# A cross network on one core: first rows in three loads, the tail's inputs moved up, padded bias sums, and the tail corner as 32x32 tiles

## The chip, the core and the metric

The kernel runs on one core of a Trainium2 chip. The metric is the device time of one execution in microseconds (us), the median of several runs. One further execution was recorded by the hardware profiler; all durations of single instructions below come from it. The core's engines are TensorE (PE in the profile, and PEld for its weight loads), VectorE (DVE), ScalarE (ACT), GpSimd (POOL) and SyncE (SP, which here only issues transfers).

## What is computed

Six layers of a cross network over 4096 rows of 416 features, all in bf16:

```python
B, F, D, L = 4096, 26, 16, 6
Din = min(F * D, 1024)          # 416
# x0: [4096, 416]   ws: [6, 416, 416]   bs: [6, 416]
def reference(x0, ws, bs):
    x = x0
    for l in range(ws.shape[0]):
        x = x0 * (x @ ws[l] + bs[l]) + x
    return x
```

The kernel uses that x is x0 times a running sum S: it keeps S in PSUM, adds each layer's product to it, and gets the next x as x0 * (S + sum of the biases).

## The kernel before

**Layout.** Features lie on partitions, rows on the free axis. The 416 features are three chunks of 128 (the "main" part, `CH`) and a tail of 32. The 4096 rows are four blocks of 1024 (`s`), and each block has two halves of 512. The sum S of a block stands in PSUM banks 0 to 5 (three chunks, two halves) and, for the tail, in banks 6 and 7 (`T_BANK`), where four quarters of 256 rows lie on the four groups of 32 partitions.

**One layer of one block** is a fixed piece of TensorE work, and there are 24 of them (six layers, four blocks; the last one is done in another form). In order:

- `main` for the first half: nine calls, each four matmuls of 128 rows of the array by 32 columns, which run side by side and stream 512 columns each;
- `tail_rows`, the 32 tail inputs: here the array is used as four groups of 32 rows, with 128 columns each. The part `first` does two chunks of 128 outputs. The part `second` does the third chunk (groups 0 and 2, 512 streamed columns each) and the *corner*, tail inputs to tail outputs, 32 by 32 (groups 1 and 3);
- `tail_outs`, main inputs to tail outputs, again 128 by 32;
- `main` for the second half.

VectorE takes every finished bank out of PSUM (`leave`, L417), ScalarE and GpSimd do the same for the tail (`leave_tail`, L427 and L440) and copy it into a second, swapped order (`swap`), because groups 1 and 3 of the array hold the other quarters' tail inputs as well.

**The corner.** `wc_sb` holds, for each layer, the 32x32 corner of the weights placed in a 128-column block that is zero elsewhere. GpSimd makes it: one memset of the whole tile (L249) and four copies for each group of layers (`corner`, L255): layer 0 early, layer 1 after layer 0 of the first block, layers 2 to 5 after layer 1. Each use is two matmuls of 256 columns in row group 1 and two in row group 3, with the zeros adding nothing to the other quarters.

**The head.** TensorE first runs 14 matmuls on constants (`fill`). The first 512 rows come by two plain loads of 256 rows (`load_rows`: rows 0 to 255 on SP's queue, 256 to 511 on ACT's) and are transposed on TensorE (L488), with six copies out of PSUM into `x0T_sb` (DVE L503, four; ACT L498, two). All later rows come by transposing loads on SP's queue (L204). In layer 0 of the first block the weights come in three pieces, and the nine `main` calls go chunk by chunk (`k`): after the first, `bias_sums` (16 small matmuls, weights `bsa_sb` of 7 partitions, against `u_sb`; ACT copies the result to `cb_sb`, L522); after the second, `tail_in(0)` (16 matmuls that transpose the tail inputs; ACT copies them to `x0t_sb`, L388).

**Order.** A small planner (`Plan`) keeps each engine's instructions in program order and puts in the semaphore waits; TensorE never passes a waiting instruction. SP issues, in order: rows 0 to 255, the three pieces of layer 0's weights, the tail inputs `xtl0` of rows 512 to 1023, the transposing load of rows 512 to 1023, and then the weights of layer 1 and on. ACT issues rows 256 to 511, the biases `bs`, and layer 0's tail weights `wt0`, and only then loads its function table.

Of the kernel before, what the change touches and what calls it, by code (L numbers as in the profile page):

```python
# [118 lines left out]
def bass_standalone__dcn_v2_cross__recsys_kernel(  # L119
# [6 lines left out]
    B, D = x0.shape  # L126
# [8 lines left out]
    G = SB // 4  # L135
# [6 lines left out]
    with ExitStack() as es:  # L142
# [5 lines left out]
        wt_sb = sb("wt_sb", [128, L, D])  # L148
        wc_sb = sb("wc_sb", [128, L, 2, 128])
        xin_sb = sb("xin_sb", [128, 4, D])  # L150
# [16 lines left out]
        dummy_sb = sb("dummy_sb", [128, 8])  # L167
        bsa_sb = sb("bsa_sb", [L + 1, D])
        u_sb = sb("u_sb", [L + 1, L])
        cb_sb = sb("cb_sb", [128, NC + 1, L], FP32)  # L170
# [23 lines left out]

        def load_rows(queue, i):
            load(queue, xin_sb[:, 2 * i:2 * i + 2, :], x0_v[:, 2 * i:2 * i + 2, :], "xin%d" % i, [("xin", i)])

# [9 lines left out]

        load_rows("sync", 0)
        load_rows("scalar", 1)
        for k in CH:  # L210
            load("sync", w_sb[:, 0, k, :], ws[0, 128 * k:128 * k + 128, :], "w0_%d" % k, [("w", 0, k)])
        load("scalar", bsa_sb[1:L + 1, :], bs[:, :], "bs", [("bs",)])
        load(
            "scalar", wt_sb[:, 0, :], ws[0, DF:D, :].unsqueeze(0).to_broadcast([4, DR, D]), "wt0", [("wt", "wt0")]
        )
        load("sync", xtl_sb[:, 4:JS, :], x0_v[:, 4:JS, DF:D], "xtl0", [("xtl", 0)])
        load_transposed(0, H, SB)
# [8 lines left out]
        for s in range(1, NS):  # L226
# [14 lines left out]
        )  # L241
        P.add("gpsimd", lambda e: e.memset(bsa_sb[0:1, :], 1.0), writes=[("bs1",)])
        P.add(
            "gpsimd", lambda e: e.affine_select(
                out=u_sb[:, :], in_=ones_sb[0:L + 1, 0:L], pattern=[[1, L]],
                compare_op=ALU.is_ge, fill=0.0, base=1, channel_multiplier=-1,
            ), reads=[("ones",)], writes=[("u",)],
        )
        P.add("gpsimd", lambda e: e.memset(wc_sb[:, :, :, :], 0.0), writes=[("wc", "wt%d" % i) for i in range(3)])  # L249

        def corner(a, b, name):
            for g in range(4):
                p = quad(g | 1)
                P.add(
                    "gpsimd", lambda e, p=p, g=g: e.tensor_copy(  # L255
                        out=wc_sb[p, a:b, g % 2, quad(g)], in_=wt_sb[p, a:b, DF:D]
                    ), reads=[("wt", name), ("wc", name)], writes=[("wc", name, g)], shifts=True,
                )


# [47 lines left out]
        def tail_rows(s, l, start):  # L308
            src, key = src_tail(s, l)
            keys = [("wt", wkey(l)), key, key + ("swapped",)]  # L310

            def rows(pe, q, h, m, begin):
                for part in range(2):
                    if q % 2 == 0:
                        if part:
                            break
                        dst, rhs = ps[:, bank(h, m), :], src[quad(q), :, :]
                    else:
                        dst, rhs = ps[:, bank(h, m), part * G:(part + 1) * G], src[quad(q), 1 - part, :]
                    ins = mm(  # L320
                        pe, dst, wt_sb[quad(q), l, m * 128:(m + 1) * 128], rhs, begin and part == 0, (32 * q, 0)
                    )
                return ins

            def first(pe):
                for q in range(4):
                    h, m = divmod(q, 2)
                    ins = rows(pe, q, h, m, l == 0 and h == 1)
                return ins

            def second(pe):
                for q in range(4):
                    h = q // 2
                    if q % 2 == 0:
                        ins = rows(pe, q, h, 2, l == 0 and h == 1)
                    else:
                        for part in range(2):
                            ins = mm(
                                pe, ps[:, T_BANK[h], 0:G], wc_sb[quad(q), l, part, :], src[quad(q), 1 - part, :],
                                start and part == 0, (32 * q, 0),  # L340
                            )
                return ins

            P.add("tensor", first, reads=keys, adds=[("ps", bank(h, m)) for h in HALVES for m in range(2)])
            P.add(
                "tensor", second, reads=keys + [("wc", wkey(l), g) for g in range(4)],
                adds=[("ps", bank(h, 2)) for h in HALVES] + [("ps", T_BANK[h]) for h in HALVES],
            )
# [18 lines left out]
        def tail_in(s):  # L367
            def fn(pe):
                for o in range(2 if s == 0 else 1):
                    for r in range(2):  # L370
                        for g in range(4):
                            j = 2 * (g ^ o) + r
                            src = xin_sb[:, j, DF:D] if s == 0 and j < 4 else xtl_sb[:, s * JS + j, :]
                            b, c = (7, o * G) if s == 0 else (T_BANK[0], G)
                            ins = mm(
                                pe, ps[quad(g), b, c + r * 128:c + (r + 1) * 128], src, ident[:, :],
                                s == 0 and o == 0 and r == 0, (0, 32 * g),
                            )
# [3 lines left out]
            P.add(  # L382
                "tensor", fn, reads=[("ident",), ("xtl", 0 if s == 0 else 1)] + ([("xin", 0), ("xin", 1)] if s == 0 else []),
                adds=[("ps", b)],
# [95 lines left out]
        B_BANK = 6  # L480
        fill(14)
        for i in range(2):
            for c in CH:
                b = HEAD_BANKS[i][c]

                def fn(pe, i=i, c=c, b=b):
                    for j in range(2):
                        ins = pe.transpose(  # L488
                            out=psT[:, b, j * 128:(j + 1) * 128],
                            in_=xin_sb[:, 2 * i + j, c * 128:(c + 1) * 128], identity=ident[:, :],  # L490
                        )
                    return ins

                P.add("tensor", fn, reads=[("xin", i), ("ident",)], adds=[("ps", b)])
                dst, src = x0T_sb[:, c, i * 256:(i + 1) * 256], psT[:, b, 0:256]
                if c == 1:
                    P.add(
# [30 lines left out]

        corner(0, 1, "wt0")
        for s in range(NS):  # L530
            for l in range(L):
# [3 lines left out]
                if s == 0 and l == 0:  # L535
                    for k in CH:
                        for m in CH:
                            main(s, l, 0, m, k)
                        if k == 0:
                            bias_sums()  # L540
                        if k == 1:
                            tail_in(0)
                    tail_rows(s, l, True)
# [14 lines left out]
                if l == 2 and s < NS - 1:  # L558
                    keep_tail_in(s + 1)
                if s == 0 and l == 0:  # L560
                    corner(1, 2, "wt1")
                if s == 0 and l == 1:
                    corner(2, L, "wt2")
                if l == 1 and s > 0:
# [156 lines left out]
```

## Time and profile before

| | |
|---|---|
| median of 3 runs | 129.16 us (128.88 to 129.17) |
| profiled execution, its own time | 129.15 us |
| its span, first to last instruction | 127.9 us |
| DVE busy | 98.2 us (77% of the span) |
| POOL busy | 39.6 us (31%) |
| DMA reads and writes | 4.07 MB and 3.41 MB of HBM |

The span is what the profiler saw between the program's first and last instruction; the remaining 1.25 us of the profiled time lie around it. A row of the timeline gives the start in us, the length in us, the engine, the line of the code, the operation, output and inputs, the shape, and how many instructions the row takes together; in square brackets stands how long the engine had been idle and what ended that. Matmuls overlap one another, so the length of a matmul row is longer than the time between the starts of two of them; what sets the pace is the distance of the starts.

The first matmuls of the program are slower than the later ones, which the timeline shows in their starts: the 14 matmuls of `fill` stream 256 columns each and begin at 0.83 us, one about every 0.21 us.

```profile
0.83 3.15 PE L270 MATMUL ps<-const-bfloat16-1.0 128*128 128x256 bf16 x14 [0.83 <-PEq L706]
```

### The profile page before, as it was taken

The numbers are of one execution on the slowest core, as the hardware profiler recorded it, in microseconds if no ns is written. First come the engines' busy times: TensorE is split into PE (matmuls) and PEld (weight loads), VectorE is DVE, ScalarE is ACT, GpSimd is POOL, SyncE is SP. The second block draws the span as 40 slices with busy tenths as digits, with TensorE's granted clock in tenths as the row PEclk, the third lists the DMA queues.
The fourth block names the chain that finished last, engine by engine and source line by source line (L and its number), as shares of the span: only waits on it lengthen the run. The fifth ranks groups of instructions, "written<-read, shape, count | busy, mean of one in ns | idle before, by whom it ended". The sixth has DMA issues, their size and how long they took to land.

```text
span 127.9 us, 5334 instructions
## 1 busy us (share of the span) xinstructions
PE 124.4 (97%) x2426; PEld 64.7 (51%) x2426; DVE 98.2 (77%) x150; ACT 50.1 (39%) x112; POOL 39.6 (31%) x88
## 2 busy tenths in 40 slices
PE   7999999999999999999999999999999999999991
PEld 5545445545545545545545545545555555455660
DVE  0329779679779779788788797797797797797973
ACT  1534226356405224354513243373422252253820
POOL 7025364034014053043122152241221351340550
PEclk9999999999999999999999999999999999999999
DMA  3987999997739307000019208000009606100016
GB/s 106 205 201 175 161 262 273 172 204 149 253 67 143 65 19 258 5 0 5 0 33 192 52 0 265 7 5 0 5 0 129 142 5 233 38 0 5 0 38 233
DMA packets 34054, 13.12 MB, mean 103 GB/s; under 512 B 25322, under 2 KB 34032, under 8 KB 34032
## 3 DMA queue, kind: packets, MB, share of 16 engines
q1 hardware_dynamic: 33328, 12.25, 45.8%
q10 hardware_dynamic: 704, 0.54, 1.3%
q8 instruction: 19, 0.31, 1.0%
q14 instruction: 3, 0.02, 0.0%
HBM read 4.07 MB, written 3.41 MB: 58 GB/s over the span
## 4 chain that ended last, share of the span: by engine, by line
PE 97%; ACT 0%; DVE 0%; issue 0%
PE ps L262 93%; PE ps L270 2%; PE ps L488 1%; ACT x0t_sb L388 0%; DVE o_sb L652 0%
## 5 line engine op out<-in xcount | busy, mean ns | idle before, releaser
L417 DVE SCALAR_TENSOR_TENSOR xT_sb<-ps,cb_sb,x0T_sb 128x512 bf16<-128x512 f32 x120 | 80.8, 743 | 19.5 <-PE ps L262 19.5
L262 PE MATMUL ps<-xT_sb,w_sb 128*32 128x512 bf16 (+1 forms) x1596 | 84.6, 364 | 0.0
L262 PEld LDWEIGHTS ps<-xT_sb,w_sb 128*32 128x32 bf16 x1596 | 40.8, 97 | 37.2 <-issue 4.0
L427 ACT ACTIVATE t_sb<-ps,cb_sb 64x256 f32<-64x256 f32 x46 | 21.6, 470 | 51.3 <-PE ps L262 51.0
L440 POOL TENSOR_TENSOR xt_sb<-t_sb,x0t_sb 128x256 bf16<-128x256 f32 x20 | 13.4, 672 | 64.1 <-ACT t_sb L427 64.1
L404 ACT ACTIVATE xt_sb<-xt_sb 32x256 bf16<-32x256 bf16 x38 | 15.7, 414 | 15.3 <-POOL xt_sb L440 15.1
L262 PE MATMUL ps<-x0T_sb,w_sb 128*32 128x512 bf16 (+1 forms) x336 | 18.9, 368 | 0.0
L406 POOL COPY xt_sb<-xt_sb 32x256 bf16<-32x256 bf16 x38 | 14.9, 392 | 2.4
L417 DVE SCALAR_TENSOR_TENSOR xo_sb<-ps,cb_sb,x0T_sb 128x512 bf16<-128x512 f32 x18 | 12.1, 743 | 2.5 <-PE ps L262 2.5
L262 PEld LDWEIGHTS ps<-x0T_sb,w_sb 128*32 128x32 bf16 x336 | 8.4, 97 | 7.6 <-issue 0.6
L262 PE MATMUL ps<-xt_sb,wt_sb 32*128 32x512 bf16 (+1 forms) x152 | 11.8, 326 | 0.0
L262 PE MATMUL ps<-xt_sb,wc_sb 32*128 32x256 bf16 x76 | 7.4, 268 | 0.0
L262 PEld LDWEIGHTS ps<-xt_sb,wt_sb 32*128 32x128 bf16 x152 | 2.5, 91 | 8.4 <-DVE xT_sb L417 6.4
L440 POOL TENSOR_TENSOR xot_sb<-t_sb,x0t_sb 128x256 bf16<-128x256 f32 x3 | 2.0, 672 | 9.9 <-ACT t_sb L427 9.9
L262 PE MATMUL ps<-w_sb,xT_sb 128*32 128x416 bf16 (+1 forms) x60 | 5.1, 339 | 0.0
L404 ACT ACTIVATE x0t_sb<-x0t_sb 32x256 bf16<-32x256 bf16 x12 | 4.9, 410 | 0.1
L652 DVE TENSOR_TENSOR o_sb<-ps,xr_sb 128x416 bf16<-128x416 f32 x6 | 3.4, 588 | 1.3 <-PE ps L262 1.0
L255 POOL COPY wc_sb<-wt_sb 32x32 bf16<-32x32 bf16 (+1 forms) x12 | 2.8, 233 | 4.7 <-DMA wt_sb<-in_ws_dram 4.1
L270 PE MATMUL ps<-const-bfloat16-1.0 128*128 128x256 bf16 x14 | 3.1, 418 | 0.8 <-PEq L706 0.8
L262 PEld LDWEIGHTS ps<-xt_sb,wc_sb 32*128 32x128 bf16 x76 | 3.7, 93 | 0.2
L503 DVE COPY x0T_sb<-ps 128x256 bf16<-128x256 bf16 x4 | 1.1, 292 | 3.4 <-PE ps L488 3.2
L449 ACT ACTIVATE sS_sb<-ps,cb_sb 128x512 bf16<-128x512 f32 x5 | 3.0, 692 | 0.0
(41 smaller groups left out, 33.6 us busy)
## 6 DMA issues: line engine op xcount, KB each, us to landing
out_dram<-o_sb SPq DMA_DIRECT2D x3, 832.0 KB, 4.4
w_sb<-in_ws_dram SPq DMA_DIRECT2D x5, 312.0 KB, 4.3
xr_sb<-in_x_dram SPq DMA_DIRECT2D x1, 832.0 KB, 5.3
wt_sb<-in_ws_dram SPq DMA_DIRECT2D x4, 104.0 KB, 2.9
out_dram<-o_sb SPq DMA_DIRECT2D x2, 208.0 KB, 2.2
w_sb<-in_ws_dram SPq DMA_DIRECT2D x3, 104.0 KB, 3.4
xin_sb<-in_x_dram ACTq DMA_DIRECT2D x1, 208.0 KB, 3.2
xin_sb<-in_x_dram SPq DMA_DIRECT2D x1, 208.0 KB, 2.9
```

The lines of the kernel that those rows point to most:

```text
L255: "gpsimd", lambda e, p=p, g=g: e.tensor_copy(out=wc_sb[p, a:b, g % 2, quad(g)], in_=wt_sb[p, a:b, DF:D]), reads=[("wt", name), ("wc", nam ...
L262: return pe.matmul(dst, lhsT=lhsT, rhs=rhs, start=start, stop=True, skip_group_check=True, tile_position=pos,)
L270: ins = pe.matmul(ps[:, 7, 0:256], lhsT=const[:, 0:128], rhs=const, start=True, stop=True)
L404: fn = lambda e, d=dst, s=src: e.activation(out=d, in_=s, func=ACTF.Copy)
L406: fn = lambda e, d=dst, s=src: e.tensor_copy(out=d, in_=s)
L417: "vector", lambda e: e.scalar_tensor_tensor(out=dst, in0=ps[:, bank(h, c), :], scalar=cb_sb[:, c, l:l + 1], in1=x0T_sb[:, c, o:o + H], op ...
L427: "scalar", lambda e, p=p, h=h: e.activation(out=dst[p, :], in_=ps[p, T_BANK[h], 0:G], func=ACTF.Identity, bias=cb_sb[p, NC, l:l + 1]), re ...
L440: "gpsimd", lambda e: e.tensor_tensor(out=dst, in0=t, in1=x0t_sb[:, s, 0, :], op=ALU.mult),
L449: fn = lambda e: e.activation(out=o, in_=i, func=ACTF.Identity, bias=b)
L488: ins = pe.transpose(out=psT[:, b, j * 128:(j + 1) * 128], in_=xin_sb[:, 2 * i + j, c * 128:(c + 1) * 128], identity=ident[:, :],)
L503: "vector", lambda e, d=dst, s=src: e.tensor_copy(out=d, in_=s),
L652: "vector", lambda e: e.tensor_tensor(out=o_sb[:, jj, :], in0=ps[:, b, 0:D], in1=xr_sb[:, j, :], op=ALU.mult), reads=[("ps", b), ("xr",)], ...
```

## The change

Four things are changed together.

- The first 512 rows come in three loads: rows 0 to 127 on SP's queue, 128 to 255 and 256 to 511 on ACT's. The transposes run row block by row block; of the six copies out of PSUM, five are now DVE's and one ACT's. `fill` has 12 matmuls.
- The tail inputs `xtl0` are loaded on ACT's queue (third, ahead of `wt0`) and no longer on SP's. In layer 0 of the first block `tail_in(0)` stands after the first chunk, and `bias_sums` after the second.
- `bsa_sb` and `u_sb` have 128 partitions. DVE clears `bsa_sb` and sets its first row to one; the biases are loaded on GpSimd's queue, after the clearing.
- The corner uses the tail weights where they lie, as tiles of 32 by 32 of the array: two matmuls of 256 columns in row group 1, into two column groups, and two in row group 3. They stand behind both 512-column matmuls of `second`. `wc_sb`, its memset and its copies are gone.

```diff
-        load_rows("sync", 0)
-        load_rows("scalar", 1)
+        load_rows("sync", 0, 1)
+        load_rows("scalar", 1, 2)
+        load_rows("scalar", 2, 4)
         for k in CH:
             load("sync", w_sb[:, 0, k, :], ws[0, 128 * k:128 * k + 128, :], "w0_%d" % k, [("w", 0, k)])
-        load("scalar", bsa_sb[1:L + 1, :], bs[:, :], "bs", [("bs",)])
+        load("scalar", xtl_sb[:, 4:JS, :], x0_v[:, 4:JS, DF:D], "xtl0", [("xtl", 0)])
         load(
             "scalar", wt_sb[:, 0, :], ws[0, DF:D, :].unsqueeze(0).to_broadcast([4, DR, D]), "wt0", [("wt", "wt0")]
         )
-        load("sync", xtl_sb[:, 4:JS, :], x0_v[:, 4:JS, DF:D], "xtl0", [("xtl", 0)])
         load_transposed(0, H, SB)
...
-        P.add("gpsimd", lambda e: e.memset(bsa_sb[0:1, :], 1.0), writes=[("bs1",)])
+        P.add("vector", lambda e: e.memset(bsa_sb[:, :], 0.0), writes=[("bs0",)])
+        P.add("vector", lambda e: e.memset(bsa_sb[0:1, :], 1.0), reads=[("bs0",)], writes=[("bs1",)])
+        P.add("gpsimd", lambda e: e.dma_start(bsa_sb[1:L + 1, :], bs[:, :]), reads=[("bs0",)], writes=[("bs",)], dma="bs")
...
-        P.add("gpsimd", lambda e: e.memset(wc_sb[:, :, :, :], 0.0), writes=[("wc", "wt%d" % i) for i in range(3)])
...
             def second(pe):
-                for q in range(4):
+                for q in (0, 2, 1, 3):
                     h = q // 2
                     if q % 2 == 0:
                         ins = rows(pe, q, h, 2, l == 0 and h == 1)
                     else:
-                        for part in range(2):
+                        for o in range(2):
+                            g = q ^ o
                             ins = mm(
-                                pe, ps[:, T_BANK[h], 0:G], wc_sb[quad(q), l, part, :], src[quad(q), 1 - part, :],
-                                start and part == 0, (32 * q, 0),
+                                pe, ps[quad(g), T_BANK[h], 0:G], wt_sb[quad(q), l, DF:D], src[quad(q), o, :],
+                                start, (32 * q, 32 * g),
                             )
...
-        fill(14)
-        for i in range(2):
+        fill(12)
+        for j in range(4):
+            i, r = divmod(j, 2)
             for c in CH:
                 b = HEAD_BANKS[i][c]
...
-                if c == 1:
+                if i and c == 2:
                     P.add(
                         "scalar", lambda e, d=dst, s=src: e.activation(out=d, in_=s, func=ACTF.Copy),
...
-        corner(0, 1, "wt0")
...
                         if k == 0:
-                            bias_sums()
-                        if k == 1:
                             tail_in(0)
+                        if k == 1:
+                            bias_sums()
...
-                if s == 0 and l == 0:
-                    corner(1, 2, "wt1")
-                if s == 0 and l == 1:
-                    corner(2, L, "wt2")
```

`tail_in` also sets the start flag on two more groups of the PSUM bank for later blocks, because the corner no longer writes them; it adds no instruction.

More of the change, by code (lines that the diff above doesn't have):

```diff
@@ L148, in bass_standalone__dcn_v2_cross__recsys_kernel @@
         wt_sb = sb("wt_sb", [128, L, D])
-        wc_sb = sb("wc_sb", [128, L, 2, 128])
         xin_sb = sb("xin_sb", [128, 4, D])
@@ L167, in bass_standalone__dcn_v2_cross__recsys_kernel @@
         dummy_sb = sb("dummy_sb", [128, 8])
-        bsa_sb = sb("bsa_sb", [L + 1, D])
-        u_sb = sb("u_sb", [L + 1, L])
+        bsa_sb = sb("bsa_sb", [128, D])
+        u_sb = sb("u_sb", [128, L])
         cb_sb = sb("cb_sb", [128, NC + 1, L], FP32)
@@ L193, in load_main, with load_rows @@
             )
-        def load_rows(queue, i):
-            load(queue, xin_sb[:, 2 * i:2 * i + 2, :], x0_v[:, 2 * i:2 * i + 2, :], "xin%d" % i, [("xin", i)])
+        def load_rows(queue, a, b):
+            load(queue, xin_sb[:, a:b, :], x0_v[:, a:b, :], "xin%d" % a, [("xin", j) for j in range(a, b)])
         def load_tail_weights(a, b, name):
@@ L241, in bass_standalone__dcn_v2_cross__recsys_kernel @@
         )
-        P.add("gpsimd", lambda e: e.memset(bsa_sb[0:1, :], 1.0), writes=[("bs1",)])
+        P.add("vector", lambda e: e.memset(bsa_sb[:, :], 0.0), writes=[("bs0",)])
+        P.add("vector", lambda e: e.memset(bsa_sb[0:1, :], 1.0), reads=[("bs0",)], writes=[("bs1",)])
+        P.add("gpsimd", lambda e: e.dma_start(bsa_sb[1:L + 1, :], bs[:, :]), reads=[("bs0",)], writes=[("bs",)], dma="bs")
         P.add(
             "gpsimd", lambda e: e.affine_select(
-                out=u_sb[:, :], in_=ones_sb[0:L + 1, 0:L], pattern=[[1, L]],
+                out=u_sb[:, :], in_=ones_sb[:, 0:L], pattern=[[1, L]],
                 compare_op=ALU.is_ge, fill=0.0, base=1, channel_multiplier=-1,
@@ L248, in bass_standalone__dcn_v2_cross__recsys_kernel @@
         )
-        P.add("gpsimd", lambda e: e.memset(wc_sb[:, :, :, :], 0.0), writes=[("wc", "wt%d" % i) for i in range(3)])
[L251 to L258, printed above, removed]
         def mm(pe, dst, lhsT, rhs, start, pos=None):
@@ L345, in tail_rows @@
             P.add(
-                "tensor", second, reads=keys + [("wc", wkey(l), g) for g in range(4)],
+                "tensor", second, reads=keys,
                 adds=[("ps", bank(h, 2)) for h in HALVES] + [("ps", T_BANK[h]) for h in HALVES],
@@ L376, in fn @@
                                 pe, ps[quad(g), b, c + r * 128:c + (r + 1) * 128], src, ident[:, :],
-                                s == 0 and o == 0 and r == 0, (0, 32 * g),
+                                o == 0 and r == 0 and (s == 0 or g >= 2), (0, 32 * g),
                             )
@@ L382, in tail_in @@
             P.add(
-                "tensor", fn, reads=[("ident",), ("xtl", 0 if s == 0 else 1)] + ([("xin", 0), ("xin", 1)] if s == 0 else []),
+                "tensor", fn, reads=[("ident",), ("xtl", 0 if s == 0 else 1)] + ([("xin", j) for j in range(4)] if s == 0 else []),
                 adds=[("ps", b)],
@@ L480, in bass_standalone__dcn_v2_cross__recsys_kernel @@
         B_BANK = 6
-        fill(14)
-        for i in range(2):
+        fill(12)
+        for j in range(4):
+            i, r = divmod(j, 2)
             for c in CH:
                 b = HEAD_BANKS[i][c]
[L486 to L494, printed above, removed]
+                P.add(
+                    "tensor", lambda pe, j=j, r=r, c=c, b=b: pe.transpose(
+                        out=psT[:, b, r * 128:(r + 1) * 128], in_=xin_sb[:, j, c * 128:(c + 1) * 128], identity=ident[:, :]
+                    ), reads=[("xin", j), ("ident",)], adds=[("ps", b)],
+                )
+                if r == 0:
+                    continue
                 dst, src = x0T_sb[:, c, i * 256:(i + 1) * 256], psT[:, b, 0:256]
-                if c == 1:
+                if i and c == 2:
                     P.add(
@@ L539, in bass_standalone__dcn_v2_cross__recsys_kernel @@
                         if k == 0:
+                            tail_in(0)
+                        if k == 1:
                             bias_sums()
-                        if k == 1:
-                            tail_in(0)
                     tail_rows(s, l, True)
```

## The prediction

> **What bounds it now.** I read the page first (who is busy), then the chain of waits (what set the end), then the timeline around one tail stage, and the head.
>
> ```profile
> PE 124.4 (97%) x2426; PEld 64.7 (51%) x2426; DVE 98.2 (77%) x150; ACT 50.1 (39%) x112; POOL 39.6 (31%) x88
> ...
> PE 97%; ACT 0%; DVE 0%; issue 0%
> PE ps L262 93%; PE ps L270 2%; PE ps L488 1%; ACT x0t_sb L388 0%; DVE o_sb L652 0%
> ```
>
> TensorE sets the end; nothing else has a percent of the chain. Told in order of time, the chain leaves TensorE just once between the first transposes and the end:
>
> ```profile
> 5.25 2.34 PE ps L262 x56
> 7.59 0.02 issue
> 7.61 0.61 ACT x0t_sb L388
> 8.22 0.05 issue
> 8.27 117.00 PE ps L262 x2240
> ```
>
> From 8.27 on, one unbroken run of 117 us. So only two things can move the time: when that run begins, and how long TensorE needs for the repeated work in it. Work taken from GpSimd is worth nothing unless TensorE waited for it.
>
> The repeated work that changes is the tail stage. One of its 23 instances (the corner rows count 76+16 = 92 matmuls, four a stage), on PE, from two windows:
>
> ```profile
> 42.36 0.39 PE L262 MATMUL ps<-xT_sb,w_sb 128*32 128x512 bf16 x4
> ...
> 42.68 0.60 PE L262 MATMUL ps<-xt_sb,wt_sb 32*128 32x512 bf16 x7
> 42.92 0.27 PE L262 MATMUL ps<-xt_sb,wc_sb 32*128 32x256 bf16 x1
> 42.92 0.37 PE L262 MATMUL ps<-xt_sb,wt_sb 32*128 32x512 bf16 x1
> 42.93 0.38 PE L262 MATMUL ps<-xt_sb,wc_sb 32*128 32x256 bf16 x3
> 43.23 0.29 PE L262 MATMUL ps<-xT_sb,w_sb 128*32 128x256 bf16 x4
> ```
>
> How long 512 columns stream: 36 of the main matmuls, nine rounds of four, fill 2.12 us with a length of 0.38, so (2.12-0.38)/8 = 0.217 us a round; 256 columns take half, 0.11. The last main round starts at 42.36 and has streamed by 42.58; the tail's first matmul starts at 42.68. **That 0.10 us is the price of changing the array from tiles of 128x32 to 32x128.** The same at the exit: the second 512-column pair starts by 42.92, has streamed by 43.14, and the 128x32 work starts at 43.23, 0.09 later. In between `first` runs into `second` with no such gap, both being 32x128. In the head the bias sums pay it too: the main round that starts at 5.87 has streamed by 6.09 and the 7x32 tiles start at 6.18, 0.09 later.
>
> ```profile
> 5.87 0.38 PE L262 MATMUL ps<-x0T_sb,w_sb 128*32 128x512 bf16 x4
> 6.18 0.11 PEld L262 LDWEIGHTS ps<-u_sb,bsa_sb 7*32 7x32 bf16 x5 [0.42 <-issue]
> ```
>
> **The corner.** Before, groups 1 and 3 each stream 2x256 columns while groups 0 and 2 stream 512, so the corner is covered: it starts at 42.92 and 43.03 and ends with the others at 43.14. Afterwards it needs only 256 columns, which by itself saves nothing, since the 512-column pair sets the end (at most 0.01 a stage). Afterwards it also is of another tile shape, 32x32 between 32x128 and 128x32, so each stage has three changes of shape in place of two. If a change of the columns alone empties the array as the others do, then: pair streamed at 43.14, corner starts at 43.23, streams 0.11 to 43.34, and the 128x32 work starts at 43.43 and not 43.23: **+0.20 us a stage, 23 x 0.20 = +4.6 us.** The trace shows changes of the rows alone (128x32 to 7x32) and of both, none of the columns alone: its one candidate, the transposes' 128x128 to 128x32 at 5.21, waits for a DVE copy. So the bounds are: -0.01 (the tiles slip into groups 1 and 3, which stand idle, and only those are emptied: their last 256 columns of `first` start at 42.81, when the corner's weight loads run, and 42.81 +0.11 +0.09 +0.11 = 43.12, before the pair is through), and +0.31 (emptied, and the two tiles of one row group one after the other, 0.11 more). I take +0.20: every change of shape that the trace has costs 0.09 to 0.10, and column tiles side by side cost one stream (four starts within 0.02 in the main rounds).
>
> The Trainium skill's page "TensorEngine Tiling (Array Packing)", section "Key Properties", says that a change of tiling mode, not merely of tile, drains the engine, and lists 32x128 and 32x32 as two modes; the gaps of 0.09 agree for row changes. By that rule this sum stands at +4.6. The page "TensorE: Matmul & The Clock Gate", section "The mechanism", lets a weight load into another row group pass running matmuls; by that alone the corner would hide and the sum would be 0.
>
> **Corner copies gone.** They delayed TensorE once. In layer 2 of the first block:
>
> ```profile
> 18.02 0.12 PEld L262 LDWEIGHTS ps<-xt_sb,wt_sb 32*128 32x128 bf16 x6 [0.42 <-POOL wc_sb L255]
> 18.40 0.09 PEld L262 LDWEIGHTS ps<-xt_sb,wt_sb 32*128 32x128 bf16 x1 [0.25 <-POOL wc_sb L255]
> ...
> 18.73 0.11 PEld L262 LDWEIGHTS ps<-xT_sb,w_sb 128*32 128x32 bf16 x6 [0.21 <-issue]
> ```
>
> The stage takes 18.73-18.02 = 0.70 against 0.55 elsewhere: **-0.15**. The rest of GpSimd's relief (2.8 us of copies, a 1.37 us memset) is idle time gained there, worth nothing.
>
> **Head, gains.** Bias sums: from 6.09 to 6.37, 0.28; padded they are 128x32 like their neighbours, four rounds of tiny matmuls, 0.13 by their own starts (6.19 to 6.29, one more round): -0.15. `tail_in` earlier: now TensorE has streamed at 7.03 and waits for `xtl0` until 7.15, -0.12 if that is there in time; and the x0t copy on ACT ends at 8.22 while the last main round has streamed by 8.04 and the shape change would allow 8.13: -0.14. Sum **-0.41**.
>
> **Head, losses.** Rows 256 to 511 move from first to second on ACT, an issue of 0.49 later; they landed 3.2 us after their issue at 0.79, so 4.0 becomes up to 4.5. The transposes begin at 3.78, behind `fill`; with two matmuls fewer that is 3.78 - 2 x 0.21 = 3.35. The first two row blocks are transposed by 3.98 (six at 0.105: twelve take 1.47 with a length of 0.31), and the third waits to 4.5; then three transposes (4.82), the copy 0.35 later (as 3.87 to 4.22 before), 0.29 long, 0.05 for the semaphore: main work at 5.5 against 5.21. If the smaller loads land sooner, DVE decides: its first copy at 3.35+0.32+0.35 = 4.02, the fourth ends at 4.02+4x0.29 = 5.18, main work at 5.23. Ends 0 and +0.3; I take +0.1, near the middle, less because the first main rounds still run slow (5.21 to 5.61 for one round) and a later start loses part of that slow time only. `xtl0`: third on ACT, issued near 1.8, wanted at about 6.2. Its landing took 4.4 on SP: 6.2. Ends: 2.1, the shortest of the tail weights' landings, gives 3.9; 5.1, what `wt0` took on ACT's queue (issue 1.98, GpSimd released at 7.07), gives 6.9 and a wait of 0.7. I take +0.06. Net head **-0.25**, from -0.45 to +0.5.
>
> **Hidden parts.** `wt0` moves behind `xtl0`, from 1.98 to about 2.55: plus 5.1 is 7.65, wanted near 7.95; bare, it would cost what it is late. SP loses one issue of 0.69, so the transposing load and every later weight load is issued 0.7 sooner: rows 512 to 1023 (3.48 plus 5.1, needed at 8.81) and layer 1's weights (6.76 plus 3.4, needed at 10.88) gain margin. ACT's table load (1.28) comes after four issues, ending near 4.5; its one copy is due at 4.9. DVE's memsets: 0.17 for 128 columns makes 0.55 for 416, twice, done by 2.2, first needed at 4.0. The bias load goes from GpSimd once DVE has cleared, near 1.6; behind it on GpSimd stands only `u_sb`'s select. The trace has no load from that queue; landings of 2.1 to 6.2 elsewhere put it at 3.7 to 7.8, wanted near 7.0: covered, or +0.8 at worst.
>
> **Sum**, against the profiled 129.15 (span 127.9 and 1.25 around it; the median is 129.16): 129.15 + 4.6 - 0.15 - 0.25 = **133.35 us**, own range 132.3 to 134.3 (0.16 to 0.21 a stage, and the head's ends).
>
> **Rivals.**
> - *The corner hides* (not slower). The 32x32 tiles run in row groups 1 and 3 while groups 0 and 2 stream. For it: those groups are idle for half of `second`, weight loads of the corner at 42.81 run while other groups stream, and `second` from group to group shows no gap. Against: each change of shape seen had a gap. Then 129.15 - 0.15 - 0.25 = 128.75 (128.3 to 129.3). It decides as soon as the step from 32x128 to 32x32 costs under 0.02 a stage.
> - *Emptied and one after the other*: +0.31 a stage, 129.15 + 7.1 - 0.4 = 135.9. Against: side by side is what the main rounds do.
> - *A load late in the head*, bias sums or tail weights, TensorE standing in order behind it: up to +1 once, 134.4 on top of the forecast. For: three loads on ACT now precede `wt0`. Against: the margins above.
>
> **Chances.** Forecast 0.62, hidden 0.27, one after the other 0.06, late load 0.05. Faster or slower by under 0.3% (0.39 us) is what a measurement here can't tell from no change. The hidden case straddles that line: 0.16 faster, 0.09 same, 0.02 slower; all others are slower, in all 0.75. Cases of both signs matter, so the range runs from the hidden case, 128.4, to the forecast's upper end, 134.3; the likeliest alone is 132.3 to 134.3.
>
> **What would show it.** In the timeline of a steady tail stage: 32x32 rows starting 0.3 after the second 512-column pair, and the distance from the stage's first matmul to the next 128x32 at 0.75, not 0.55. The hidden case shows the 32x32 rows within 0.1 of that pair and 0.55 kept. One after the other shows two starts 0.11 apart in a row group. In the head: bias sums without an idle PEld of 0.4 ahead of them, no ACT piece in the chain near 7.6, and the run of tail stages beginning near 8.0. The prediction is wrong if the stage stays at 0.55, or if the run begins after 8.5.

## The result

The changed kernel takes **135.05 us** (median of 6 runs, 134.36 to 135.44) against 129.25 us for the kernel before (median of 6, 128.88 to 129.65): a ratio of 1.043, 95% interval 1.040 to 1.046. It is slower. The direction and the main mechanism were forecast; the time lies above the forecast 133.35 and above the range's end, 134.3. The profiled execution took 134.69 us with a span of 133.4, so 5.5 us more span than before. Ratios here and below leave out single executions that took over 1.5% longer than the fastest of their kernel.

The page of the changed kernel: the engines' busy times, and the chain of waits by engine and by line.

```profile
PE 128.4 (96%) x2424; PEld 62.1 (47%) x2424; DVE 99.0 (74%) x153; ACT 49.7 (37%) x111; POOL 36.0 (27%) x75
...
PE 92%; DMA 4%; ACTq 1%; DVE 0%; issue 0%
PE ps L252 92%; DMA xtl_sb<-in_x_dram 4%; ACTq L187 1%; DVE o_sb L636 0%
```

TensorE still sets the end, but a new 4% stands in the chain: the load of the tail inputs `xtl0`. (Line numbers moved: the matmuls are now L252, the loads L187.) GpSimd gave up 3.6 us of work; all that this bought is the 0.15 us of waiting told below, as TensorE had waited for GpSimd's copies in one stage only. The chain of the same kernel in order of time (start, length, what):

```profile
1.72 5.54 DMA xtl_sb<-in_x_dram
7.27 0.14 issue
7.41 123.41 PE ps L252 x2339
```

The chain no longer runs from the fill through the transposes, as before; it goes back to ACT's third load, issued at 1.72, landed at 7.27. Two windows of the timeline show where the 5.5 us went. The first is a steady tail stage, weight loads on PEld:

```profile
44.86 0.12 PEld L252 LDWEIGHTS ps<-xt_sb,wt_sb 32*128 32x128 bf16 x8 [0.42 <-issue]
45.41 0.10 PEld L252 LDWEIGHTS ps<-xt_sb,wt_sb 32*32 32x32 bf16 x4 [0.42 <-issue]
45.62 0.88 PEld L252 LDWEIGHTS ps<-xT_sb,w_sb 128*32 128x32 bf16 x28
```

The stage lasts from 44.86 to 45.62, 0.76, in place of 0.55. The 32x32 loads begin 0.55 after the stage's start, which is exactly where the old stage ended: the corner is simply appended, 0.21 long. The mean over the 23 stages is 0.7587, against 0.5493 over the 22 others of before, so 23 x 0.209 = 4.8; the one slow stage of before (0.70, layer 2 of the first block) had 0.15 of waiting that is gone: **+4.66 us**.

The second is the head of the changed kernel, rows on PE:

```profile
5.58 0.83 PE L252 MATMUL ps<-x0T_sb,w_sb 128*32 128x512 bf16 x12 [0.20 <-DVE x0T_sb L492]
7.41 0.23 PE L252 MATMUL ps<-ident,xin_sb 128*32 128x128 bf16 x2 [0.99 <-DMA xtl_sb<-in_x_dram]
...
7.62 0.83 PE L252 MATMUL ps<-x0T_sb,w_sb 128*32 128x512 bf16 x12
...
8.27 0.27 PE L252 MATMUL ps<-u_sb,bsa_sb 128*32 128x6 bf16 x16
8.38 0.83 PE L252 MATMUL ps<-x0T_sb,w_sb 128*32 128x512 bf16 x12
9.14 0.83 PE L252 MATMUL ps<-x0t_sb,wt_sb 32*128 32x512 bf16 x12
```

The first chunk starts at 5.58 and has streamed by 6.23 (three rounds of 0.217). TensorE then does nothing until 7.41, when `tail_in` can begin: 1.18 us of waiting, of which the row counts 0.99 because it reckons the last matmul's modelled end. The first tail stage begins at 9.14; before it was 8.27: **+0.87 us**. Together 4.66 + 0.87 = 5.53, the whole difference of the spans.

The load behind that wait finishes in 16 completion parts. Their landing times in the trace of the changed kernel, in us:

```
xtl0, issued 1.72:   13 parts from 4.52 to 5.21, then 7.00, 7.10, 7.27
wt0 (broadcast), issued 2.25:   4 parts, 6.91, 6.92, 7.15, 7.37
transposing load, issued 2.66:   16 parts from 8.59 to 8.79
```

Most of `xtl0` was there two microseconds before TensorE was let go. Three late parts held it.

### The profile page after: what moved, and what is told of

Same layout as the page of the kernel before. It is cut to its first block, busy times and chain, and to the rows that moved or that the text cites. A ratio compares the mean times of both kernels' runs of the same rounds, so it can differ in the third digit from the quotient of the medians.

```text
span 133.4 us, 5312 instructions
## 1 busy us (share of the span) xinstructions
PE 128.4 (96%) x2424; PEld 62.1 (47%) x2424; DVE 99.0 (74%) x153; ACT 49.7 (37%) x111; POOL 36.0 (27%) x75
## 3 DMA queue, kind: packets, MB, share of 16 engines
HBM read 4.07 MB, written 3.41 MB: 56 GB/s over the span
## 4 chain that ended last, share of the span: by engine, by line
PE 92%; DMA 4%; ACTq 1%; DVE 0%; issue 0%
PE ps L252 92%; DMA xtl_sb<-in_x_dram 4%; ACTq L187 1%; DVE o_sb L636 0%
## 5 line engine op out<-in xcount | busy, mean ns | idle before, releaser
L252 PE MATMUL ps<-xT_sb,w_sb 128*32 128x512 bf16 (+1 forms) x1596 | 84.6, 364 | 0.0
L252 PEld LDWEIGHTS ps<-xT_sb,w_sb 128*32 128x32 bf16 x1596 | 40.8, 97 | 35.5
L252 PE MATMUL ps<-x0T_sb,w_sb 128*32 128x512 bf16 (+1 forms) x336 | 18.6, 364 | 0.2 <-DVE x0T_sb L492 0.2
L252 PE MATMUL ps<-xt_sb,wt_sb 32*128 32x512 bf16 (+2 forms) x228 | 15.7, 310 | 0.0
L252 PEld LDWEIGHTS ps<-x0T_sb,w_sb 128*32 128x32 bf16 x336 | 8.4, 97 | 7.2 <-DVE x0T_sb L492 0.4
L252 PEld LDWEIGHTS ps<-xt_sb,wt_sb 32*128 32x128 bf16 (+1 forms) x228 | 4.2, 90 | 16.1 <-issue 16.1
L252 PE MATMUL ps<-w_sb,xT_sb 128*32 128x416 bf16 (+1 forms) x60 | 5.1, 339 | 0.0
L252 PE MATMUL ps<-x0t_sb,wt_sb 32*128 32x512 bf16 (+2 forms) x48 | 3.3, 310 | 0.0
L252 PEld LDWEIGHTS ps<-w_sb,xT_sb 128*32 128x32 bf16 (+1 forms) x60 | 2.2, 97 | 1.4 <-issue 0.2
L647 POOL TENSOR_TENSOR o_sb<-f_sb,xr_sb 128x416 bf16<-128x416 f32 x2 | 1.9, 973 | 2.9 <-ACT f_sb L643 2.9
```

What stands on the lines that cost most here:

```text
L252: return pe.matmul(dst, lhsT=lhsT, rhs=rhs, start=start, stop=True, skip_group_check=True, tile_position=pos,)
L647: "gpsimd", lambda e: e.tensor_tensor(out=o_sb[:, jj, :], in0=t, in1=xr_sb[:, j, :], op=ALU.mult),
```

## The experiments

Each is a kernel of its own; the kernel before was timed beside it on the same chip, and ratios are against that.

**The corner alone.** The kernel before with only `second` and the corner's code from the change.

```diff
-                for q in range(4):
+                for q in (0, 2, 1, 3):
...
-                                pe, ps[:, T_BANK[h], 0:G], wc_sb[quad(q), l, part, :], src[quad(q), 1 - part, :],
-                                start and part == 0, (32 * q, 0),
+                                pe, ps[quad(g), T_BANK[h], 0:G], wt_sb[quad(q), l, DF:D], src[quad(q), o, :],
+                                start, (32 * q, 32 * g),
...
```

> The kernel before with the 32x32 corner alone (order 0, 2, 1, 3), the head untouched. Theory (a change from 32x128 to 32x32 empties the whole array): the tail stage takes 0.76 as in the changed kernel, 23 x 0.21 - 0.15 = +4.7, so 133.9 us, and the run of tail stages begins at 8.27. Rival (the long stage of the changed kernel comes from its head, for instance from the weights' or inputs' arrival): the stage stays at 0.55 and the time at 129.2 or a little under.

Measured: 133.94 us against 129.03, ratio 1.036 (1.033 to 1.040). One tail stage of it in the timeline, PE for the start and PEld for the two changes:

```profile
44.29 0.83 PE L249 MATMUL ps<-xt_sb,wt_sb 32*128 32x512 bf16 x12
...
44.83 0.10 PEld L249 LDWEIGHTS ps<-xt_sb,wt_sb 32*32 32x32 bf16 x4 [0.42 <-issue]
45.05 1.53 PEld L249 LDWEIGHTS ps<-xT_sb,w_sb 128*32 128x32 bf16 x40
```

0.76 again, with the old head. So the corner costs its 0.21 a stage whatever the head does; 4.9 of the 5.8 us between the medians are here. Not all of this run's loss is the corner's: the first tail stage began at 8.56 and not at the 8.27 expected, because the first twelve main matmuls, with nothing changed ahead of them, took from 5.22 to 6.62 where before they took from 5.21 to 6.19. The end of the slow starting pace thus differs from one execution to the next.

**The head alone.** The changed kernel with the zero-padded corner, its memset and its copies put back.

```diff
-                for q in (0, 2, 1, 3):
+                for q in range(4):
...
+        corner(0, 1, "wt0")
...
```

> The changed kernel with the zero-padded 128-column corner back, so only the head is changed. Theory: 135.05 - 4.7 = 130.4 us (130.0 to 131.0), stage 0.55, the first tail stage near 9.1. Rival (the head is as good as predicted and the rest of the loss belongs to the corner): 128.7 to 129.0.

Measured: 130.05, 131.1, 131.37 and 132.31 us, ratio 1.011 (1.004 to 1.017); the median, 131.23, is a little above what was expected. The steady tail stage is 0.549 again, so the head's parts, meant to shorten it, cost time on their own. The fastest execution is 1.0 us above before, near the 0.87 by which the head of the changed kernel is late. The others lose more, and the profiled one (131.37) shows how. Its timeline on PE, then windows (stretch, us, busy time of PE, PEld, DVE, ACT and POOL, granted TensorE clock, DMA share, GB/s):

```profile
7.06 0.24 PE L265 MATMUL ps<-ident,xin_sb 128*32 128x128 bf16 x2 [0.94 <-DMA xtl_sb<-in_x_dram]
...
7.39 1.53 PE L265 MATMUL ps<-x0T_sb,w_sb 128*32 128x512 bf16 x12
...
10.24 0.74 PE L265 MATMUL ps<-x0t_sb,wt_sb 32*128 32x512 bf16 x7
```

```profile
5.29:6.50 1.21, 0.83 (x12) 0.22 (x12) 0.14 (x1) 0.15 (x1) 0.00 (x0) 1.00 0.98 93
...
7.20:8.50 1.30, 1.30 (x28) 0.77 (x24) 0.00 (x0) 0.60 (x1) 0.64 (x4) 0.50 1.18 292
8.50:10.24 1.74, 1.74 (x33) 0.49 (x26) 0.00 (x0) 0.19 (x1) 0.00 (x0) 0.50 1.08 312
...
10.92:15.00 4.08, 4.08 (x88) 2.15 (x84) 3.97 (x6) 1.77 (x4) 2.10 (x7) 1.00 0.82 104
```

After the wait the granted clock is 0.50, and twelve main matmuls take 1.28 (7.39 to 8.67) instead of 0.65. None of the six executions of the changed kernel shows this; their mean clock is 1.0. So this loss is no part of the 5.8, only a risk that the same wait carries.

**`xtl0` back on SP's queue**, right ahead of the transposing load.

```diff
-        load("scalar", xtl_sb[:, 4:JS, :], x0_v[:, 4:JS, DF:D], "xtl0", [("xtl", 0)])
...
+        load("sync", xtl_sb[:, 4:JS, :], x0_v[:, 4:JS, DF:D], "xtl0", [("xtl", 0)])
         load_transposed(0, H, SB)
```

> The changed kernel with the tail inputs' load back on SP's queue, behind layer 0's weights and ahead of the transposing load. Theory (its completion is held up while the transposing load runs, whichever queue it came by): it still lands near 7, TensorE waits for it from 6.2 to about 7.1, and the time is that of the changed kernel within 0.3 (134.7 to 135.4). Rival (ACT's queue is what made it late): it lands near 6.2 or before, the wait is gone, and the time falls by about 1 us to 134.0.

Measured: 134.51 us, ratio 1.043 (1.038 to 1.049), 0.2 under the range expected. Issued at 2.66, almost a microsecond later than on ACT, it landed at 6.96. So going back to SP's queue doesn't cure it, and with this set of loads the landing hardly moved although the issue did.

**The transposing load one place later**, behind layer 1's weights.

```diff
-        load_transposed(0, H, SB)
         load_main(1)
+        load_transposed(0, H, SB)
```

> The changed kernel with the transposing load of rows 512 to 1023 issued behind layer 1's weights. Theory (the transposing load holds up the completions of loads in flight beside it): all 16 parts of the tail inputs' load land by about 5.3 to 5.8, tail_in starts behind the first main chunk near 6.25, and the wait moves to the transposed rows, wanted near 8.9; total between 133.8 and 135.5 by when those land. Rival (the four DMA engines that carry the broadcast tail weights are late by themselves): the tail inputs still land near 7.

Measured: 134.55 us, ratio 1.043 (1.038 to 1.048). `xtl0` landed at 6.42: sooner, but not at 5.3 to 5.8. The wait moved. Rows on PE of this kernel:

```profile
6.55 0.23 PE L252 MATMUL ps<-ident,xin_sb 128*32 128x128 bf16 x2 [0.30 <-DMA xtl_sb<-in_x_dram]
...
8.29 0.83 PE L252 MATMUL ps<-x0t_sb,wt_sb 32*128 32x512 bf16 x12
...
9.47 2.45 PE L252 MATMUL ps<-x0T_sb,w_sb 128*32 128x256 bf16 x48 [0.35 <-DMA x0T_sb<-in_x_dram]
```

The first tail stage begins at 8.29, 0.85 sooner than in the changed kernel, but now the transposed rows are late: the next 128x32 work starts at 9.47 and not 0.76 after the stage's start, at 9.05. So 0.4 of the gain is given back; the remaining 0.43 is what the median shows (0.5).

**`wt0` as four loads** of 32 partitions in place of one broadcast.

```diff
-        load(
-            "scalar", wt_sb[:, 0, :], ws[0, DF:D, :].unsqueeze(0).to_broadcast([4, DR, D]), "wt0", [("wt", "wt0")]
-        )
+        for q in range(4):
+            load("scalar", wt_sb[quad(q), 0, :], ws[0, DF:D, :], "wt0", [("wt", "wt0")])
```

> The changed kernel with layer 0's tail weights in four loads of 32 partitions in place of one broadcast load, whose completion comes in only four parts. Theory (four DMA engines that carry the broadcast load alone, 32 rows of 832 bytes each, hold up the last parts of the tail inputs' load and stall the transposing load): all 16 parts of the tail inputs' load land by 5.4, tail_in starts at about 6.25, the first tail stage at about 8.0 to 8.2, time 134.0. Rival (the transposing load alone holds up completions): the last parts still land at 7 and the time stays at 134.5 to 135.4.

Measured: 134.18 us, ratio 1.036 (1.033 to 1.040), so 0.9 better than the changed kernel and near the 134.0 expected, though not step by step as expected. `xtl0` landed at 6.02 and not by 5.4, `tail_in` ran at 6.16, and the first tail stage began at 8.51 and not at 8.0 to 8.2, since `wt0` itself came later. PE row, and a row of the chain:

```profile
8.51 0.83 PE L251 MATMUL ps<-x0t_sb,wt_sb 32*128 32x512 bf16 x12 [0.54 <-DMA wt_sb<-in_ws_dram]
```

```profile
3.85 4.52 DMA wt_sb<-in_ws_dram
```

The fourth of the loads is issued only at 3.85 and lands at 8.37. Both neighbours of `xtl0`, the transposing load and the broadcast, therefore seem to have a part in its delay, and neither is the whole of it.

**The first rows in two loads again**, with the fill and the copies out of PSUM of before; everything else of the change kept. `xtl0` so becomes ACT's second load and not its third.

```diff
-        load_rows("sync", 0, 1)
-        load_rows("scalar", 1, 2)
+        load_rows("sync", 0, 2)
         load_rows("scalar", 2, 4)
...
-        fill(12)
+        fill(14)
...
```

> The changed kernel with the first rows in two loads of 256 again (with the 14 fill matmuls and the copies of before); corner, bias sums and the tail inputs' place stay changed. The tail inputs are then second on ACT's queue, not third. Theory (what decides is whether a load's last parts land before the transposing load gets going near 5; one place further ahead does it): all parts land by 4.8, tail_in starts behind the first chunk near 6.1, the first tail stage near 8.0, and the time is 135.05 - 1.1 = 133.5 to 133.9 with little spread. Rival (the three row loads are no part of it): the tail inputs land near 7, 134.5 to 135.4.

Measured: 134.17 us, ratio 1.039 (1.036 to 1.043), above the 133.5 to 133.9 expected. `xtl0`, issued at 1.33 and so 0.4 sooner, landed at 4.54, 2.7 sooner. Rows on PE:

```profile
5.19 0.83 PE L251 MATMUL ps<-x0T_sb,w_sb 128*32 128x512 bf16 x12 [0.25 <-DVE x0T_sb L493]
5.84 0.22 PE L251 MATMUL ps<-ident,xin_sb 128*32 128x128 bf16 x2
...
6.45 0.83 PE L251 MATMUL ps<-x0T_sb,w_sb 128*32 128x512 bf16 x12 [0.21 <-DMA w_sb<-in_ws_dram]
...
7.70 0.83 PE L251 MATMUL ps<-x0T_sb,w_sb 128*32 128x512 bf16 x12 [0.34 <-DMA w_sb<-in_ws_dram]
8.47 0.83 PE L251 MATMUL ps<-x0t_sb,wt_sb 32*128 32x512 bf16 x12
```

`tail_in` follows the first chunk without a gap. But TensorE now waits twice for the second and third piece of layer 0's weights, whose last parts landed at 6.41 and 7.66, so that 0.67 of the 0.87 is recovered and not all.

All thirteen traces side by side show what was wrong with pricing this load by a fixed duration (landing of its last part, us):

| kernel | `xtl0` issued | landed |
|---|---|---|
| before | 2.75, SP | 7.11 |
| corner alone | 2.75, SP | 6.84 |
| changed | 1.72, ACT third | 7.27 |
| same load order (head alone; order 0,1,2,3; all 32x32; wait filled) | 1.72 to 1.73 | 6.93, 6.98, 7.78, 7.23 |
| back on SP | 2.66, SP | 6.96 |
| transposing load later | 1.73 | 6.42 |
| `wt0` in four loads | 1.73 | 6.02 |
| rows in two loads (here, and the two last experiments) | 1.32 to 1.33, ACT second | 4.54, 4.64, 4.55 |

**The order of `second`.** The two kernels that follow are about the array. The changed kernel, with the quarters in their old order, so that 32x128 and 32x32 alternate.

```diff
-                for q in (0, 2, 1, 3):
+                for q in range(4):
```

> The changed kernel with the second part of the tail stage in the order 0, 1, 2, 3, so that the 32x32 pairs stand between the 32x128 matmuls. Theory (each change of shape empties the whole array): the stage becomes 512 columns, 256, 512, 256, each with its gap of 0.09: 0.53 more a stage than with the pairs at the end less the overlap, so about 1.15 to 1.3 a stage and 144 to 147 us. Rival (only the row group concerned is emptied, and the 0.21 has another cause): the stage stays at 0.76 and the time at 135.

Measured: 147.66 us, one execution. One tail stage on PEld (a row names the shape of its first load; the second row also holds the 32x128 load that follows the corner's first pair):

```profile
44.07 0.12 PEld L252 LDWEIGHTS ps<-x0t_sb,wt_sb 32*128 32x128 bf16 x7 [0.42 <-issue]
44.60 0.30 PEld L252 LDWEIGHTS ps<-x0t_sb,wt_sb 32*32 32x32 bf16 x3 [0.41 <-issue]
45.13 0.09 PEld L252 LDWEIGHTS ps<-x0t_sb,wt_sb 32*32 32x32 bf16 x2 [0.23 <-issue]
45.34 0.66 PEld L252 LDWEIGHTS ps<-x0T_sb,w_sb 128*32 128x32 bf16 x24
```

1.27 a stage, as forecast; the time is a little above the 144 to 147 expected. In this execution the granted clock was 0.50 from 7.04 to 10.46, as in the head alone, and the first tail stage began at 10.33, 1.2 later than in the changed kernel. From 44.60 to 45.13 stand a corner pair (0.21) and a 512-column matmul all by itself (0.31 = 0.217 + 0.09); nothing overlaps, though the two are in different row groups. A change of the tile's columns alone empties the whole array, not the row group that changes.

**The whole tail stage in 32x32 tiles**, so that the shape does not change inside it.

```diff
-                    ins = mm(
-                        pe, dst, wt_sb[quad(q), l, m * 128:(m + 1) * 128], rhs, begin and part == 0, (32 * q, 0)
-                    )
+                    for c in range(4):
+                        f0 = m * 128 + 32 * c
+                        ins = mm(
+                            pe, dst[quad(c)], wt_sb[quad(q), l, f0:f0 + 32], rhs, begin and part == 0, (32 * q, 32 * c)
+                        )
```

> The changed kernel with the whole tail stage in 32x32 tiles: every 32x128 matmul becomes four of 32x32 beside one another, same inputs, same sums. Theory (the change of shape inside the stage is what costs): no change of shape inside, the stage goes back to 0.55 to 0.60 although it has four times as many instructions, and the time falls by 23 x 0.16 to 0.21 to 130.2 to 131.4. Rival (32x32 tiles are slow, or the corner's place at the end is what costs): 0.76 or more, 135 or more.

Measured: 132.04 us, ratio 1.019 (1.014 to 1.023): much faster than the changed kernel, but above the 130.2 to 131.4 expected. One stage on PEld:

```profile
45.88 0.23 PEld L252 LDWEIGHTS ps<-xt_sb,wt_sb 32*32 32x32 bf16 x33 [0.42 <-DVE xT_sb L410]
46.30 0.10 PEld L252 LDWEIGHTS ps<-xt_sb,wt_sb 32*32 32x32 bf16 x3 [0.19 <-issue]
46.52 0.34 PEld L252 LDWEIGHTS ps<-xT_sb,w_sb 128*32 128x32 bf16 x16
```

0.64 a stage: 0.115 of the 0.209 comes back, about the price of one change of shape. What is left, 0.09, is about what the corner's own 256 columns take; they still run behind the others. Why the corner's last loads wait until 46.30 with no change of shape ahead of them isn't shown.

**The wait filled.** The head alone, with ten matmuls on constants (they compute nothing that is used) between the first chunk and `tail_in`.

```diff
                         if k == 0:
+                            fill(10)
                             tail_in(0)
```

> The changed head with the old corner (as in e2_head_alone), and ten matmuls on constants between the first chunk and tail_in, 1.1 us of work that fills the wait for the tail inputs and computes nothing. Theory (the wait of about 1 us lets the clock of TensorE fall to half for some 3.4 us, which made three of four executions of e2 slower by 1 to 2 us): granted clock 1.0 in all executions, 129.9 to 130.6. Rival (the clock falls for another reason): executions at 0.987 and 131 to 132 as before.

Measured: 130.43 us (130.01, 130.38, 130.48, and 133.49), ratio 1.008 (1.005 to 1.011); mean clock given as 1.0 in all. Three of four lie near the best of the head alone, which agrees with the clock having fallen for the wait there; four executions are few, and it is not shown beyond that. The fourth is the profiled one; two of its rows on PE:

```profile
7.78 2.31 PE L273 MATMUL ps<-const-bfloat16-1.0 128*128 128x256 bf16 x10
...
11.85 0.81 PE L265 MATMUL ps<-x0T_sb,w_sb 128*32 128x512 bf16 x12
```

Here TensorE had stood idle for 1.18 already before its transposes (rows 256 to 511 landed at 5.33), and the matmuls went at the slow starting pace, ten of 256 columns in about 2.2 us, until the chunk at 11.85. The trace of this execution holds no record of the granted clock at all, and the column then reads 1.00, so the expected "1.0 in all" is not borne out by it.

**A better version.** The old corner; rows in two loads; `xtl0` second on ACT; padded bias sums behind `tail_in`; `wt0` in four loads; and the corner copies of layers 2 to 5 one layer at a time.

```diff
...
-                if s == 0 and l == 1:
-                    corner(2, L, "wt2")
+                if s == 0 and 1 <= l < L - 1:
+                    corner(l + 1, l + 2, "wt2")
```

> A version meant to beat both: the kernel before with its row loads, fill and copies and its zero-padded corner, and of the change only the padded bias sums and the tail inputs on ACT's queue with tail_in ahead of the second chunk; layer 0's tail weights in four loads, the corner copies one layer at a time. Theory: bias -0.15, tail inputs -0.12, their copy -0.14, corner wait -0.15 give 129.05 - 0.56 = 128.5 (128.2 to 128.8). Rival (the tail inputs still land at 7): 129.6 to 130.5, and the clock may drop in the wait.

Measured: 129.55 us, ratio 1.001 (0.999 to 1.003): no gain, where 128.2 to 128.8 was expected. The stage of layer 2 is 0.549, as hoped, and `xtl0` landed at 4.64; but `wt0` lands at 7.71, and GpSimd, which copies the corner from it, is late:

```profile
7.77 1.01 POOL L256 COPY wc_sb<-wt_sb 32x32 bf16<-32x32 bf16 x4 [3.89 <-DMA wt_sb<-in_ws_dram]
```

The first tail stage starts at 8.08 and stands half done until the copies end at 8.78.

**The same with `wt0` as one broadcast again.**

```diff
-        for q in range(4):
-            load("scalar", wt_sb[quad(q), 0, :], ws[0, DF:D, :], "wt0", [("wt", "wt0")])
+        load(
+            "scalar", wt_sb[:, 0, :], ws[0, DF:D, :].unsqueeze(0).to_broadcast([4, DR, D]), "wt0", [("wt", "wt0")]
+        )
```

> The version of e9_best with layer 0's tail weights in one broadcast load again, since the four loads landed at 7.7 and held up the corner's copies and the first tail stage by 0.62. Theory: tail inputs still land by 4.8 (second on ACT's queue), the tail weights near 6.9, corner copies done by 8.1, no wait in the first tail stage, which starts near 8.0 in place of 8.27; with the corner wait of layer 2 gone as in e9: 0.25 + 0.15 faster than before, ratio 0.996 to 0.998. Rival (the tail weights land at 7.7 too): ratio 1.000 or above.

Measured: **128.94 us** (12 runs) against 129.25 (17 runs), ratio 0.997 (0.995 to 0.999): faster than both kernels, by 0.3%. On PE, the head and its first tail stage:

```profile
6.37 0.22 PE L264 MATMUL ps<-ident,xin_sb 128*32 128x128 bf16 x2
...
8.09 0.60 PE L264 MATMUL ps<-x0t_sb,wt_sb 32*128 32x512 bf16 x7
```

The first tail stage begins 0.18 sooner than before and 0.15 is saved in layer 2: about 0.3, the measured difference. The first part comes from what is kept of the change, the padded bias sums and the earlier tail inputs, which weren't tried apart; the second comes from the smaller copies, which are no part of the change. The slow starting pace lasted longer here than in the trace of before (`tail_in` waits for the first chunk until 6.37; before, the bias sums began at 6.19), so that the head's own gain is more than the 0.18 that is seen.

## Why the prediction was wrong

**The corner, right.** It put +0.20 on each of 23 stages, by the rule that every change of shape costs 0.09 to 0.10 and that a change of the columns alone, which no row of before showed, would too. Measured: 0.209 a stage, and the kernel with the corner alone is 4.9 us slower, some 0.3 of it from its slower start. The bound below (the corner slips into idle row groups) fell: the alternating order shows the whole array empty each time. The bound above (two tiles of a row group one after the other) fell too. The Trainium skill's page "TensorEngine Tiling (Array Packing)", section "Key Properties", says that a change of mode drains the engine; the runs agree, now for a change of columns alone as well, at about 0.1 us. The page "TensorE: Matmul & The Clock Gate", section "The mechanism", which lets weight loads of other row groups run ahead, gave 0 for the corner; that does not hold here once the shapes differ: the 32x32 loads at 45.41 came after 0.42 without a weight load.

**The corner copies, right.** -0.15: the stage of layer 2 has no wait left, here and, by smaller copies, in the last two experiments.

**The head's gains, right.** Forecast -0.41. The bias sums take 0.11 in place of 0.28 (-0.17); the wait for `xtl0` ahead of the old `tail_in` (0.12) is gone from there, though it came back larger ahead of the new one, as told below; and between the last chunk and the tail stage stand 0.11 in place of 0.23 (-0.12). Again -0.41.

**The start of the main work, right in sum.** It was put 0.1 later, with +0.3 as the end. It came 0.37 later, at 5.58, but the first chunk then ran at full pace, 0.65 and not 0.88: together +0.14. That a later start loses only part of the slow time was in the working; that the two came out at +0.14 is partly luck, as the start itself was later than the stated end and the slow pace lasts differently long from one execution to the next (the corner alone has the head of before and kept it 0.4 longer).

**`xtl0`, the step that failed.** The prediction says: "Its landing took 4.4 on SP: 6.2 ... I take +0.06", with 6.9 and a wait of 0.7 as the worst end. It landed at 7.27, 5.5 after its issue, and TensorE waited 1.18: the term put at 0.06 measured 1.18. That one term makes the head +0.87 and not -0.25, and takes the sum from 133.35 to 134.5 for the profiled execution, beside its 134.69; the corner's 0.009 a stage is the other 0.2. The head's stated upper end, +0.5, was also added up too low: -0.41 with the ends of 0.3 and 0.7 is +0.6. The measured head, +0.87, lies beyond that too.

The fault lies in treating the landing as an issue time plus a duration. The trace of before already had this load landing at 7.11, and TensorE waiting 0.12 for it:

```profile
2.75 0.69 SPq L188 DMA_DIRECT2D xtl_sb<-in_x_dram  x1
...
7.15 0.10 PEld L262 LDWEIGHTS ps<-ident,xin_sb 128*32 128x32 bf16 x2 [0.44 <-DMA xtl_sb<-in_x_dram]
```

In the table above, issues a microsecond apart on two queues land between 6.84 and 7.27 in seven of the first eight traces, and in the changed kernel the load's last part (7.27) comes about when its neighbours' do (the third weight piece 6.91, the broadcast 7.37). The prediction moved the *consumer* of the load from behind the second chunk to behind the first, 0.8 us forward (wanted at 6.23, before at 7.03), and let the load follow by arithmetic. A cautious reading would have kept the landing at 7.1 and charged about 0.9 for the wait, 134.2, with a range past 135.

What is shown: with one row load fewer ahead of it, and so issued 0.4 us sooner, it landed 2.3 to 3.2 sooner than in the five kernels with the change's order of loads, in all three kernels that tried it; which of the two counts was not tried apart. The transposing load and the broadcast each seem to hold it back, by 0.5 to 1.4 and 0.9 to 1.8 against those five; these are single traces, and five of one order spread over 0.85 by themselves. The packets of the load (512 of 64 bytes) show that the landings near 7 on the two queues come about differently. On SP the data itself was late: the last packet ended at 6.76 in before (landed 7.11) and at 6.55 with the load back on SP (6.96). In the changed kernel the last one ended at 4.90, and only the completion came at 7.27. Not shown is how a few parts are held when the data is through.

With two row loads it was a weight piece that came late (7.66, issued at 2.27); in the last experiment, with the same order of these loads, that piece was there by 6.57. Which load is hit, then, isn't settled by the order alone. The Trainium skill's page "DMA: Bandwidth & Descriptors", section "Queues, rings and completion order", states that a completion count from one DMA engine is written only after all earlier writes of that engine, across its queues. Three late parts of sixteen, with the data through and landing among the broadcast's four, are what that would look like; but in the trace with all 32x32 tiles six parts came after 6.7, more than the broadcast has parts, and no run here follows a single DMA engine. So the cause of the late parts stays open.

**The rivals.** The hidden corner is excluded. "A load late in the head", 134.4 with a chance of 0.05, was the right kind of event at a wrong place: it named the bias sums and the tail weights, both of which were covered (the biases landed at 5.04, `wt0` at 7.37 with 9.14 as the time of need), and not the tail inputs, whose use had been moved forward. The prediction's own mark, "or if the run begins after 8.5", is what happened.

The medians are not quite the profiled executions: 135.05 beside 134.69. That 0.36 is spread between runs, and no trace tells more of it; with the two terms above (1.12 and 0.2) it adds up to the 1.7 between the forecast and the median.

## What to carry to other kernels

Count the changes of tile shape on TensorE ahead of counting streamed columns: here each cost about 0.1 us, whatever part of the array it concerned, and work that hid in idle row groups stopped hiding as soon as its shape differed. When a consumer is moved forward past a load, ask when the load *lands* in the trace and what else is in flight then, rather than adding a duration to a new issue time. A part that is worth 0.2 us once in the head should be tried apart from one that is paid in every layer.

## What was unexpected in the hardware

- A load of 32 KB had 13 of its 16 parts there by 5.21 and the last at 7.27, although its last data packet had ended at 4.90, while a broadcast load (four parts, 6.91 to 7.37) and a transposing load (8.79) were in flight.
- In four traces (the head alone, `xtl0` back on SP, the order 0, 1, 2, 3, and all 32x32) the granted clock was 0.50 for 3.41 us, from the last part of TensorE's wait for the tail inputs or just behind it; in the head alone from 7.16 to 10.57. A wait of 1.18 in the changed kernel had no such effect in six executions. The clock's records begin with a stretch at 1.00; of its first 3.41 us TensorE was idle, by its rows, for 1.65 to 1.89 in those four traces, and for 1.19 in the changed kernel, the most of the other eight traces that have a record. Idle time summed over the stretch thus tells the traces apart, where the length of the one wait (1.01 to 1.89 against 1.18) does not. No experiment varied it by itself.
- The granted-clock column reads 1.00 wherever the trace has no record of the clock. The first record stands at 3.6 to 6.6 us in twelve traces, at 5.69 in before, and the matmuls ahead of it ran at about half pace (256 columns in 0.21 us, against the steady 0.11). With the wait filled there is no record in the whole trace, and 256 columns still took 0.22 us past 9 us.
